# Chunk-selected attention and a hard-swish layer: K and Q of the quads in longer rows, bounds in three column groups, batch 0's high bounds in four, a new order

## The chip, the cores and the metric

The kernel runs on one core of one Trainium2 chip. The metric is the device time of one execution in microseconds; for each kernel the median of several runs is given. A profiled execution gives the trace from which the views of the profile are taken.

## What is computed

Attention over 4 batches, 8 heads, 768 tokens of 64 elements, in which each query attends to at most 6 chunks of 32 keys, followed by a layer without biases. Per head:

```python
k_min, k_max = k_chunks.min(axis=3), k_chunks.max(axis=3)      # 24 chunks of 32 keys
ub = sum(maximum(q * k_min, q * k_max), axis=-1)               # an upper bound for each query and chunk
ub = where(chunk of the query >= chunk, ub, -1e9)
sel = the 6 chunks with the highest ub
scores = where(sel & causal, scale * q @ k.T, -1e9)
out = softmax(scores) @ v
```

The heads are put side by side (3,072 rows of 512), and then

```python
h = x @ w_in                                                   # 512 -> 2048
y = (h * clip(h + 3, 0, 6) / 6) @ w_out                        # 2048 -> 512
```

The first 192 queries see at most 6 chunks, so no selection is needed for them; bounds and masks are made for queries 192 to 767.

## The kernel before

**Order.** One list of tokens, `ORDER`, is walked once (line 660). Each token calls one function, which issues the instructions of one step. A token names the step, its numbers, and the PSUM buffer that it writes: a, b, c are two banks each (`PSB`), x and y one bank each (`PSS`; a, b and c can serve so too). Each engine runs its instructions in the order in which they were issued and waits on semaphores for what they read and for buffers to be free. The list therefore fixes the order on each engine and on each DMA queue, SP's above all.

**Batch 0, pairs of heads** (tokens in capitals). A pair i has 128 partitions, 64 for each head. K and Q are loaded by halves of 384 tokens (`LK`, `LQ`, `AQ`, 96 KB each), turned on TensorE (`KT`, `QT`), reduced to chunk maxima and minima on VectorE (`MX`, `MN`), cast on ScalarE (`KB`, `QB`). The bounds are two products, of the positive part of q (`RP`) with the maxima and of the negative part (`RN`) with the minima: `UH.i.h`, with h 0 for the first 192 queries that need a selection and 1 for the other 384. Then a bias add (`UB`), a turn on TensorE (`TH`), the eight largest (`T8`), the comparison with the sixth (`SE`), the turn back (`LH`), and a copy (`MT`). `S` computes scores in six units, to which a matmul with a constant adds -8192 where a chunk was not chosen.

**Batches 1 to 3, quads of heads** (small letters; n is 2 to 7, four heads on 32 partitions each). `lk.n` and `lq.n` load K and Q, four DMAs of 192 KB each: partition t of a head gets tokens t, t+32, t+64 and so on, in rows of 256 bytes. `kd` and `qd` turn 32x32 blocks on VectorE in place, so that 32 elements of the head dimension lie along partitions. Each step has two halves. `mx` and `mn` reduce K to chunk maxima and minima, and `kx` subtracts them; `kb` and `qb` cast to bf16 on ScalarE; `rp` makes the positive part of q. With max(q a, q b) = q b + relu(q)(a - b), the bounds (`ud.n.c.cc`) are 64 small matmuls in 4 row and 4 column groups of the TensorE array, 144 queries in each column group. After them come, for two heads at a time, bias add (`us`), turn (`tr`), top-8 (`tm`, nine `max`), comparison (`se`) and turn back (`tb`), all on VectorE, and then `mv.n.g`, GpSimd copies that bring the rows of head g to its 32 partitions. `SQ.n.u` computes scores and mask of the four heads for unit u.

**All batches.** `ex` exponentiates scores on ScalarE, `af` applies the causal mask on GpSimd, `A` and `B` multiply by the values (low and high half), `na` and `nb` normalise on VectorE. x is turned into `XT` by TensorE (`X`, with the copy `xe` on VectorE) or by DMA transposes on SP's queue (`xt`). Per group g of 384 rows, `H.g.f` are eight blocks of 8 matmuls with `w_in`, `hu` and `gt` the gate on ScalarE and VectorE, `O.g.t.n` four blocks of 4 matmuls with `w_out` for each of three tiles, `ot` the eviction and `st` the store. Weights are loaded by `wl` and cast on GpSimd by `wc`; values by `LV`/`VC` and `lv`/`vc`.

**Staging.** K and Q of the quads share three slabs of `STAGE`; a load waits until everything that read the slab's last content is done.

Of the kernel before, what the change touches and what calls it, by code (L numbers as in the profile page):

```python
# [15 lines left out]
P = 128  # L16
# [30 lines left out]
KB.3.1 S.3.1.b ex.3.1 S.3.0.c LQ.3.1.0 LV.1.0.0 LQ.3.1.1 QT.3.1.x MX.3.1 RN.3.1 ex.3.0 VC.1.0 af.2.0 A.1.y na.1
RP.3.1 LH.2.1.b MT.2.1 S.1.3.a ex.1.3 S.1.4.c LV.2.0.0 kd.2.1 X.0.0.y xe.0.0 ex.1.4 UH.3.1.b UB.3.1 af.3.1 mx.2.1
S.1.5.a S.1.2.c QB.3.1 VC.3.0 af.3.0 A.3.y na.3 LV.2.0.1 ex.1.5 af.1.3 ex.1.2 VC.2.0 A.2.x S.0.2.b ex.0.2 TH.3.1.y
na.2 S.2.3.c ex.2.3 T8.3.1 LV.0.1.1 SE.3.1 wl.0 S.2.5.a X.0.1.x xe.0.1 S.2.2.b ex.2.2 LH.3.1.y MT.3.1 wc.0 af.0.2  # L50
wl.1 kd.2.0 mx.2.0 H.0.1.c hu.0.1 ex.2.5 gt.0.1 mn.2.0 af.1.2 af.0.3 LV.0.1.0 VC.0.1 B.0.0.x H.0.0.b hu.0.0 gt.0.0
wc.1 B.0.1.x nb.0 H.0.2.c hu.0.2 mn.2.1 gt.0.2 S.3.3.b ex.3.3 S.3.2.a ex.3.2 LV.1.1.1 LV.1.1.0 VC.1.1 kb.2.1 af.1.5
kb.2.0 wl.2 wc.2 B.1.0.y B.1.1.y nb.1 lk.3 S.3.5.b af.3.2 kd.3.1 mn.3.1 bd ex.3.5 af.3.5 H.0.4.c hu.0.4 gt.0.4
mx.3.1 H.0.3.a S.2.4.b af.2.2 ex.2.4 kd.3.0 kx.2 mx.3.0 wl.3 H.0.5.c hu.0.5 gt.0.5 hu.0.3 af.2.5 lq.2 gt.0.3 wc.3
H.0.6.b hu.0.6 S.3.4.c qd.2.1 af.3.3 ex.3.4 LV.3.1.0 H.0.7.a gt.0.6 af.2.3 rp.2.1 qd.2.0 LV.3.1.1 VC.3.1 LV.2.1.1
X.1.0.c xe.1.0 B.3.0.x LV.2.1.0 B.3.1.x kb.3.0 VC.2.1 B.2.0.y B.2.1.y nb.3 rp.2.0 ud.2.c.b nb.2 hu.0.7 wl.4 gt.0.7
X.1.1.x xe.1.1 H.1.3.a hu.1.3 us.2.1 qb.2.0 us.2.0 tr.2.1 H.1.1.b hu.1.1 tm.2.1 wc.4 mn.3.0 O.0.0.0.y se.2.1 gt.1.3
gt.1.1 tb.2.1 mv.2.3 lq.3 qd.3.0 qd.3.1 wl.5 H.1.6.c kb.3.1 hu.1.6 gt.1.6 O.0.2.0.x tr.2.0 kx.3 H.1.5.a hu.1.5
qb.2.1 wc.5 mv.2.2 H.1.2.b hu.1.2 rp.3.1 gt.1.5 H.1.0.c rp.3.0 O.0.0.1.y gt.1.2 tm.2.0 hu.1.0 gt.1.0 O.0.2.1.x
qb.3.0 wl.6 wc.6 se.2.0 ud.3.b.a tb.2.0 mv.2.1 mv.2.0 us.3.1 tr.3.1 H.1.7.c hu.1.7 lv.5 wl.7 us.3.0 lk.4 H.1.4.a  # L60
wc.7 hu.1.4 vc.5 gt.1.7 tm.3.1 O.0.2.2.x SQ.2.5.c.b lq.4 ex.5.5 gt.1.4 qb.3.1 O.0.0.2.y SQ.2.4.b.a ex.4.5 af.4.5
ex.5.4 se.3.1 tb.3.1 mv.3.3 O.0.2.3.x ot.0.2 tr.3.0 tm.3.0 O.0.0.3.y se.3.0 tb.3.0 ex.4.4 mv.3.1 kd.4.1 mx.4.1
ot.0.0 SQ.2.0.a.c ex.4.0 kd.4.0 mn.4.0 ex.5.0 mv.3.2 mv.3.0 O.0.1.0.x O.0.1.1.x qd.4.1 SQ.2.3.b.a O.0.1.2.x ex.5.3
qd.4.0 lv.4 ex.4.3 O.0.1.3.x ot.0.1 SQ.2.1.c.a ex.4.1 af.4.1 st.0.0 O.1.0.0.y O.1.0.1.y lv.7 rp.4.1 ex.5.1
SQ.2.2.c.b O.1.0.2.y vc.4 af.5.5 rp.4.0 ex.5.2 mn.4.1 mx.4.0 kx.4 af.4.3 af.4.0 A.4.x na.4 af.5.0 qb.4.0 st.0.1
ex.4.2 ud.4.b.a af.5.1 kb.4.0 st.0.2 af.5.2 us.4.0 O.1.0.3.y us.4.1 vc.7 tr.4.1 ot.1.0 tm.4.1 SQ.3.1.c.b O.1.2.0.x
ex.7.1 ex.6.1 kb.4.1 SQ.3.0.a.b se.4.1 ex.6.0 lv.6 ex.7.0 lk.5 tr.4.0 tm.4.0 A.5.y O.1.2.1.x SQ.3.4.c.a af.6.1
ex.7.4 vc.6 af.6.0 na.5 A.6.y O.1.2.2.x na.6 af.4.2 tb.4.1 kd.5.1 af.7.1 SQ.3.3.a.b ex.6.4 lv.8 af.7.0 ex.6.3 A.7.y
X.2.0.c O.1.2.3.x xe.2.0 ex.7.3 SQ.3.5.a.c ot.1.2 na.7 ex.6.5 X.2.1.b xe.2.1 B.4.0.x B.4.1.x af.5.3 B.5.0.y kd.5.0
se.4.0 mx.5.0 ex.7.5 mn.5.0 B.5.1.y qb.4.1 mv.4.3 H.2.2.b nb.5 nb.4 H.2.0.a hu.2.2 hu.2.0 gt.2.2 st.1.0 H.2.3.c  # L70
# [41 lines left out]
def kernel(  # L112
# [104 lines left out]
    def load_rows(m, x):  # L217
        def issue(n, *only):
            b, first = divmod(4 * n, H)
            dst = staged(m, n).rearrange("p h n x t -> p (h n) (x t)")  # L220
            for g in only or range(4):
                nc.sync.dma_start(dst[CH * g:CH * (g + 1)], x[b, first + g].rearrange("(n t) d -> t n d", t=CH))
# [470 lines left out]
```

## Time and profile before

| what | us |
|---|---|
| median of 3 runs | 278.69 (277.73 to 280.13) |
| the profiled execution | 275.69 |
| its span, first to last instruction | 274.0 |
| TensorE busy in it | 261.3 |
| VectorE busy | 184.0 |
| ScalarE busy | 181.0 |
| GpSimd busy | 102.6 |

The granted clock of TensorE was 1.000 over the whole span. A busy time counts an instruction from its start to its end, and matmuls overlap, so the busy time of TensorE is not a measure of its peak. Line numbers (L333) are those of the kernel before; PE, DVE, ACT, POOL and SP are TensorE, VectorE, ScalarE, GpSimd and the sync engine; PEld is the loading of weights, and a q behind an engine means its sequencer or queue. The moved bytes were 36.08 MB in 91,479 DMA packets, 84,144 of them under 512 bytes.

### The profile page before, as it was taken

The numbers are of one execution on the slowest core, as the hardware profiler recorded it, in microseconds if no ns is written. First come the engines' busy times: TensorE is split into PE (matmuls) and PEld (weight loads), VectorE is DVE, ScalarE is ACT, GpSimd is POOL, SyncE is SP. The second block draws the span as 40 slices with busy tenths as digits, with TensorE's granted clock in tenths as the row PEclk, the third lists the DMA queues.
The fourth block names the chain that finished last, engine by engine and source line by source line (L and its number), as shares of the span: only waits on it lengthen the run. The fifth ranks groups of instructions, "written<-read, shape, count | busy, mean of one in ns | idle before, by whom it ended". The sixth has DMA issues, their size and how long they took to land.

```text
span 274.0 us, 8574 instructions
## 1 busy us (share of the span) xinstructions
PE 261.3 (95%) x3550; PEld 153.7 (56%) x3550; DVE 184.0 (67%) x452; ACT 181.0 (66%) x249; POOL 102.6 (37%) x241
## 2 busy tenths in 40 slices
PE   6998997899999999999999999998999999999994
PEld 3666765565545565664545655464655565555561
DVE  4898998999899779867874788575662423342620
ACT  2798978647499894878578746992887634325610
POOL 7215686325777552532825232421544310000000
PEclk9999999999999999999999999999999999999999
DMA  8999999998996999139900449114212044003002
GB/s 164 205 180 163 335 250 252 219 286 246 261 184 190 160 212 186 36 76 171 231 4 28 107 103 173 40 21 99 79 52 47 2 133 100 0 2 115 38 22 97
DMA packets 91479, 36.08 MB, mean 132 GB/s; under 512 B 84144, under 2 KB 84400, under 8 KB 91440
## 3 DMA queue, kind: packets, MB, share of 16 engines
q1 hardware_dynamic: 89040, 34.94, 56.6%
q10 hardware_dynamic: 2400, 0.59, 1.2%
q8 instruction: 28, 0.46, 0.8%
q14 instruction: 11, 0.09, 0.1%
HBM read 27.26 MB, written 6.29 MB: 122 GB/s over the span
## 4 chain that ended last, share of the span: by engine, by line
PE 76%; DMA 13%; SPq 3%; DVE 3%; POOL 1%; ACT 1%; issue 1%; DVEq 0%
PE PSy L625 15%; PE PSx L625 10%; PE PBa L587 10%; PE PBc L587 9%; PE PBb L587 8%; DMA WS<-in_moe_w_in_dram 4%; DMA STAGE<-in_q_dram 4%; DMA STAGE<-in_k_dram 3%; PE PBa L510 3%; PE PSx L543 2%; PE PSy L543 2%; PE PBc L625 2%; PE PBc L510 2%; PE PBb L510 2%; PE PBb L333 2%; DMA XT<-XB 1%
## 5 line engine op out<-in xcount | busy, mean ns | idle before, releaser
L587 PEld LDWEIGHTS <-WIN 128*128 128x128 bf16 x512 | 48.9, 98 | 37.7 <-issue 4.2
L527 POOL TENSOR_SCALAR_AFFINE_SELECT PT<-PT 128x256 bf16<-128x256 bf16 x78 | 30.2, 409 | 70.2 <-ACT PT L520 69.9
L625 PEld LDWEIGHTS <-GT 128*128 128x128 bf16 x368 | 33.1, 98 | 37.8 <-issue 2.4
L625 PE MATMUL PSy<-WOUT,GT 128*128 128x512 bf16 x192 | 46.8, 380 | 0.0
L363 POOL COPY MQ<-MTM 32x144 bf16<-32x144 bf16 x96 | 29.1, 304 | 31.3 <-DVE MTM L357 27.5
L587 PE MATMUL PBc<-XT,WIN 128*128 128x384 bf16 x184 | 33.7, 326 | 1.4 <-DVE GT L598 1.4
L598 DVE SCALAR_TENSOR_TENSOR GT<-U,PBa 128x768 bf16<-128x768 bf16 x22 | 20.9, 948 | 19.8 <-ACT U L595 19.8
L587 PE MATMUL PBa<-XT,WIN 128*128 128x384 bf16 x176 | 32.4, 326 | 1.3 <-DMA XT<-XB 0.7
L625 PE MATMUL PSx<-WOUT,GT 128*128 128x512 bf16 x128 | 31.8, 380 | 0.0
L598 DVE SCALAR_TENSOR_TENSOR GT<-U,PBc 128x768 bf16<-128x768 bf16 x23 | 21.8, 947 | 10.4 <-ACT U L595 10.3
L520 ACT ACTIVATE PT<-PBb 128x1024 bf16<-128x1024 f32 (+2 forms) x26 | 23.6, 908 | 7.6 <-PE PBb L514 5.3
L587 PE MATMUL PBb<-XT,WIN 128*128 128x384 bf16 x152 | 27.8, 326 | 0.2 <-POOL WIN L242 0.2
L595 ACT ACTIVATE U<-PBc 128x768 bf16<-128x768 f32 x23 | 18.7, 812 | 13.9 <-PE PBc L587 10.2
L598 DVE SCALAR_TENSOR_TENSOR GT<-U,PBb 128x768 bf16<-128x768 bf16 x19 | 18.1, 951 | 13.6 <-ACT U L595 13.6
L595 ACT ACTIVATE U<-PBa 128x768 bf16<-128x768 f32 x22 | 17.9, 812 | 13.5 <-PE PBa L587 13.5
L520 ACT ACTIVATE PT<-PBc 128x1024 bf16<-128x1024 f32 (+2 forms) x26 | 24.2, 930 | 3.5 <-PE PBc L497 1.3
L520 ACT ACTIVATE PT<-PBa 128x1024 bf16<-128x1024 f32 (+2 forms) x26 | 23.9, 921 | 3.8 <-PE PBc L514 2.0
L228 DVE STREAM_TRANSPOSE STAGE<-STAGE 128x768 f32<-128x768 f32 x24 | 22.7, 960 | 1.7 <-DMA STAGE<-in_k_dram 1.3
L595 ACT ACTIVATE U<-PBb 128x768 bf16<-128x768 f32 x19 | 15.4, 812 | 12.1 <-PE PBb L587 12.1
L311 DVE TENSOR_REDUCE KMA<-STAGE 128x24 f32<-128x768 f32 x24 | 22.3, 941 | 0.1
L543 PEld LDWEIGHTS <-PT 128*128 128x128 bf16 x546 | 19.0, 97 | 3.6 <-issue 0.7
L510 PEld LDWEIGHTS <-KBA 32*128 32x128 bf16 x480 | 9.4, 92 | 14.7 <-issue 11.7
(192 smaller groups left out, 460.3 us busy)
## 6 DMA issues: line engine op xcount, KB each, us to landing
out_dram<-OT SPq DMA_DIRECT2D x23, 256.0 KB, 2.5
STAGE<-in_k_dram SPq DMA_DIRECT2D x24, 192.0 KB, 5.0
STAGE<-in_q_dram SPq DMA_DIRECT2D x24, 192.0 KB, 5.5
VS<-in_v_dram SPq DMA_DIRECT2D x12, 384.0 KB, 4.2
WS<-in_moe_w_in_dram SPq DMA_DIRECT2D x4, 1024.0 KB, 7.0
WS<-in_moe_w_out_dram SPq DMA_DIRECT2D x4, 1024.0 KB, 6.7
STAGE<-in_k_dram SPq DMA_DIRECT2D x16, 96.0 KB, 3.2
VS<-in_v_dram SPq DMA_DIRECT2D x16, 96.0 KB, 4.2
```

The source lines that it names most:

```text
L228: nc.vector.transpose(out=T, in_=T)
L311: nc.vector.tensor_reduce(out=dst, in_=staged("k", n)[:, h], axis=AX.X, op=(A.max, A.min)[w])
L333: nc.tensor.matmul(PSB[(c, cc)[g // 2]][CH * part:CH * (part + 1), g % 2, 0:NQ // 4], lhsT=KM4[n % 2][rows, w, x, :], rhs=R[rows, :, x, 8 ...
L363: nc.gpsimd.tensor_copy(MQ[n % 2][CH * g:CH * (g + 1), w * part:w * (part + 1)], MT4[n % 2][CH * part:CH * (part + 1), w * g:w * (g + 1)])
L510: nc.tensor.matmul(PSB[both[g // 2]][:, g % 2, at:at + w], lhsT=K[rows, x, j * P:(j + 1) * P], rhs=Q[rows, x, q0:q0 + w], start=(x == 0), ...
L520: nc.scalar.activation(pt(i, u)[:, :, 0:n], PSB[slot["S", i, u]][:, :, 0:n], ACT.Exp, scale=float(scale))
L527: nc.gpsimd.affine_select(out=T[:, :, lo:lo + P], in_=T[:, :, lo:lo + P], pattern=[[0, 2], [1, P]], compare_op=A.is_ge, fill=0.0, base=0, ...
L543: nc.tensor.matmul(O[:, e, t, :], lhsT=pt(i, u)[:, e, lo:lo + P], rhs=VB[i % 4][:, j, e, :], start=(j == 0), stop=(j == qb))
L587: nc.tensor.matmul(PSB[c][:, ff, 0:GRP], lhsT=WIN[:, kt, (2 * f + ff) * P:(2 * f + ff + 1) * P], rhs=XT[g % 3][:, kt, :], start=(kt == 0), ...
L595: nc.scalar.activation(slot["R", g, f][:], PSB[slot["H", g, f]][:, :, 0:GRP], ACT.Relu, bias=3.0)
L598: nc.vector.scalar_tensor_tensor(out=GT[g % 2][:, 2 * f:2 * f + 2, :], in0=slot["R", g, f][:], scalar=6.0, in1=PSB[slot["H", g, f]][:, :, ...
L625: nc.tensor.matmul(PSS[c], lhsT=GT[g % 2][:, f, t * P:(t + 1) * P], rhs=WOUT[:, f, :], start=(f == 0), stop=(f == FT - 1))
```

## The change

- Quads: K is loaded with 4 consecutive tokens a partition (rows of 1,024 bytes), Q with 6 (1,536 bytes). After the turn the tokens lie in another order, which each reader takes into account: `kb` and `qb` are two casts of half the size instead of one, and write tokens 4 or 6 elements apart; `mx` and `mn` are two reduces, over two axes.
- Bounds of the quads: three column groups of 192 queries instead of four of 144, so 48 matmuls instead of 64, whose right-hand sides are contiguous. Bias add, turn, comparison and turn back work on 96 partitions and 384 columns (before 128 and 288), top-8 has 12 `max` a step instead of 9, and the turn is made in place. `mv.n.g` is 3 copies of 192 that put the queries back in order, instead of 4 of 144; the mask matmul then reads contiguous columns.
- Batch 0, h = 1: bounds in four column groups of 96 (16 matmuls instead of 8), a bias add on 128 partitions and 192 columns (before 64 and 384), two turns instead of four.
- The order is new throughout. The low half of batch 1's x (group 2) is turned by `xt.2`, DMA transposes, where before it was `X.2.0`, `X.2.1` on TensorE with two copies on VectorE. `bd`, the bias of the quads, is now among the first steps. Otherwise the list has the same steps.

```diff
+    RUN = {"k": 4, "q": 6}
+    NP3 = NQ // 3
+    def slab(m, n):
+        at = (1 + 2 * (n - FIRST_QUAD) + "kq".index(m)) % 3
+        return FLAT[:, 2 * S * at:2 * S * (at + 1)]
     def staged(m, n):
-        at = (1 + 2 * (n - FIRST_QUAD) + "kq".index(m)) % 3
-        return STAGE[:, 2 * at:2 * at + 2].rearrange("p h (n x t) -> p h n x t", x=2, t=CH)
+        return slab(m, n).rearrange("p (u r x t) -> p x u r t", r=RUN[m], x=2, t=CH)
...
-                nc.sync.dma_start(dst[CH * g:CH * (g + 1)], x[b, first + g].rearrange("(n t) d -> t n d", t=CH))
+                nc.sync.dma_start(dst[CH * g:CH * (g + 1)], x[b, first + g].rearrange("(u t r) d -> t u (r d)", t=CH, r=RUN[m]))
...
+    def first_query(h, g):
+        return Q0 * (h + 1) + (96, Q0)[h] * (g % 2) + 96 * (g // 2)
...
-            dst = (KB4 if m == "k" else QB4)[n % 2][:, :, SH * h:SH * (h + 1)].rearrange("p x (n t) -> p n x t", t=CH)
...
+            dst = (KB4 if m == "k" else QB4)[n % 2].rearrange("p x (u t r) -> p x u r t", t=CH, r=RUN[m])
+            n_u = S // (2 * CH * RUN[m])
+            for x in range(2):
+                out, src = dst[:, x, n_u * h:n_u * (h + 1)], staged(m, n)[:, x, n_u * h:n_u * (h + 1)]
...
     def chunk_bounds(w):
         def issue(n, h):
-            dst = KM4[n % 2][:, w, :, NCH // 2 * h:NCH // 2 * (h + 1)].rearrange("p x n -> p n x")
-            nc.vector.tensor_reduce(out=dst, in_=staged("k", n)[:, h], axis=AX.X, op=(A.max, A.min)[w])
+            for x in range(2):
+                src = staged("k", n)[:, x, 3 * h:3 * h + 3].rearrange("p u r (c t) -> p u c r t", t=CH // RUN["k"])
+                dst = KM4[n % 2][:, w, x, NCH // 2 * h:NCH // 2 * (h + 1)].rearrange("p (u c) -> p u c", c=4)
+                nc.vector.tensor_reduce(out=dst, in_=src, axis=AX.XY, op=(A.max, A.min)[w])
...
-                for part in range(4):
+                for part in range(3):
                     for g in range(4):
                         rows = slice(CH * g, CH * (g + 1))
-                        nc.tensor.matmul(PSB[(c, cc)[g // 2]][CH * part:CH * (part + 1), g % 2, 0:NQ // 4],
-                                         lhsT=KM4[n % 2][rows, w, x, :], rhs=R[rows, :, x, 8 * part:8 * part + 8],
+                        R = raw[rows, x, part + 1] if w else RPA[rows, x, NP3 * part:NP3 * (part + 1)]
+                        nc.tensor.matmul(PSB[(c, cc)[g // 2]][CH * part:CH * (part + 1), g % 2, 0:NP3],
+                                         lhsT=KM4[n % 2][rows, w, x, :], rhs=R,
...
-        for s in range(9):
-            nc.vector.max(out=T8D[:, 9 * p + s, :], in_=bounds_rows(p)[:, s, :])
+        for s in range(12):
+            nc.vector.max(out=T8D[0:96, 12 * p + s, :], in_=bounds_rows(p)[:, s, :])
...
-        for part in range(4):
-            w = NQ // 4
-            nc.gpsimd.tensor_copy(MQ[n % 2][CH * g:CH * (g + 1), w * part:w * (part + 1)],
-                                  MT4[n % 2][CH * part:CH * (part + 1), w * g:w * (g + 1)])
+        for part in range(3):
+            lo = NP3 * part
+            nc.gpsimd.tensor_copy(MQ[n % 2][CH * g:CH * (g + 1), lo:lo + NP3].rearrange("p (t r) -> p r t", t=CH),
+                                  MT3[(2 * n + g // 2) % 3][CH * part:CH * (part + 1), NP3 * (g % 2):NP3 * (g % 2 + 1)]
+                                  .rearrange("p (r t) -> p r t", t=CH))
...
     def bounds_half(i, h, c):
-        n = 96 * (h + 1)
         for m, R in enumerate((RP, RN)):
-            for g in range(2):
-                lo = Q0 * h + n * g
+            for g in range(2 * (h + 1)):
+                lo = first_query(h, g) - Q0
...
-                                 rhs=chosen[rows, (lo - Q0) // CH:(q0 + w - Q0) // CH], start=False, stop=True,
+                                 rhs=MQ[n % 2][rows, lo - Q0:q0 + w - Q0], start=False, stop=True,
```

The part of the new order around the bounds of quad 4, as the prediction speaks of it:

```diff
-SQ.2.2.c.b O.1.0.2.y vc.4 af.5.5 rp.4.0 ex.5.2 mn.4.1 mx.4.0 kx.4 af.4.3 af.4.0 A.4.x na.4 af.5.0 qb.4.0 st.0.1
-ex.4.2 ud.4.b.a af.5.1 kb.4.0 st.0.2 af.5.2 us.4.0 O.1.0.3.y us.4.1 vc.7 tr.4.1 ot.1.0 tm.4.1 SQ.3.1.c.b O.1.2.0.x
+af.4.1 mv.3.3 kb.4.0 kb.4.1 af.5.3 tb.3.0 mv.3.0 mv.3.1 vc.6 mn.4.1 mn.4.0 O.1.0.0.y O.1.0.1.y lv.7 mx.4.1 vc.7
+mx.4.0 kx.4 ud.4.b.a kd.5.1 mx.5.1 qb.4.0 af.4.5 us.4.1 O.1.0.2.y SQ.3.1.a.c A.4.x ex.6.1 af.6.1 tr.4.1 ex.7.1
+us.4.0 SQ.3.0.a.b na.4 ex.6.0 af.5.1 A.5.x O.1.0.3.y na.5 mn.5.1 ex.7.0 ot.1.0 st.0.0 af.4.3 SQ.3.4.a.c af.6.0
```

More of the change, by code (lines that the diff above doesn't have):

```diff
@@ L208 @@
     IDENTB = const.tile([P, P], BF16, name="IDENTB")
[L209 to L211 removed]
+    BIASM = const.tile([P, 2, 96], FP32, name="BIASM")
+    BIASH = [BIASM[0:64, 0], BIASM[:, 1]]
+    BIAS3 = const.tile([96, NP3], FP32, name="BIAS3")
     EM = const.tile([P, NBLK, 2, P], BF16, name="EM")
```

243 lines of the change are left out of this document (118 added, 125 removed).

## Prediction

> **What bounds the kernel now.** I read the page first, then the windows, the chain of waits, and last single groups and stretches of the timeline. On the page the share of TensorE says how little there can be to win, and the slices say where.
>
> ```profile
> span 274.0 us, 8574 instructions
> PE 261.3 (95%) x3550; PEld 153.7 (56%) x3550; DVE 184.0 (67%) x452; ACT 181.0 (66%) x249; POOL 102.6 (37%) x241
> DVE  4898998999899779867874788575662423342620
> DMA  8999999998996999139900449114212044003002
> GB/s 164 205 180 163 335 250 252 219 286 246 261 184 190 160 212 186 36 76 171 231 4 28 107 103 173 40 21 99 79 52 47 2 133 100 0 2 115 38 22 97
> ```
>
> TensorE is busy 95% of the span. A slice is 6.85 us: in the first 13 (to 89 us) VectorE and the DMA engines are also near full, and after that both fall off. I cut the windows at the events that matter below.
>
> ```profile
> 0.00:9.84 9.84, 6.78 (x50) 4.25 (x53) 5.10 (x21) 3.60 (x8) 7.14 (x17) 1.00 1.00 180
> 9.84:40.00 30.16, 28.57 (x470) 20.05 (x460) 29.05 (x105) 25.70 (x42) 13.71 (x27) 1.00 0.95 229
> 40.00:52.42 12.42, 9.76 (x114) 6.20 (x114) 10.58 (x17) 9.57 (x12) 7.33 (x12) 1.00 1.09 220
> 52.42:60.00 7.58, 7.15 (x217) 5.52 (x216) 7.07 (x14) 3.18 (x6) 2.90 (x3) 1.00 1.12 271
> 60.00:89.22 29.22, 29.22 (x386) 15.25 (x390) 27.22 (x70) 22.91 (x32) 19.67 (x45) 1.00 0.90 229
> 89.22:259.85 170.63, 169.94 (x2282) 96.90 (x2282) 103.11 (x227) 114.05 (x149) 51.83 (x139) 1.00 0.42 89
> ```
>
> Columns: length, then PE, PEld, DVE, ACT and POOL busy, granted clock, DMA share, GB/s. From 89 us on TensorE lacks 0.7 us of 170.6 while VectorE is 60% busy: there only TensorE's own work counts. Up to 89 us three things are full at once. Which one decides is in the chain of waits, and in what VectorE waited for:
>
> ```profile
> 44.62 7.67 DMA STAGE<-in_q_dram
> 52.42 0.98 DVE STAGE L228
> 55.73 0.31 PE PBc L333 x2
> ```
> ```profile
> DVE STAGE L228 <- DMA STAGE<-in_k_dram: 1.3, 1, 1.3
> DVE STAGE L228 <- DMA STAGE<-in_q_dram: 0.5, 1, 0.5
> ```
>
> The first quad's Q lands at 52.29 us, is turned on VectorE, and its bounds start on TensorE at 55.73. So the chain runs through the loads, but VectorE, which the data goes to, waited for them only 1.8 us in all. It had other work. That is the point of this case: the loads are late, but VectorE is nearly as full as they are.
>
> **The loads (gain, mostly covered).** Before 52.29 us three quad loads of 4 x 192 KB run (K of quads 2 and 3, Q of 2): 2.36 MB in 256-byte rows. At the 180 GB/s of the first window, where all is 256-byte rows, that is 13.1 us; at the 335 GB/s of the fifth slice, which has 2,048-byte weight rows in it, 7.0. Longer rows lie between, so 3 to 6 us of DMA time go. The new order issues four 96 KB V loads ahead of quad 2's Q that stood behind it (0.39 MB, 2.1 us at 180), so this Q lands 1 to 4 us earlier. SP gains too:
>
> ```profile
> 42.00 4.87 SPq L222 DMA_DIRECT2D STAGE<-in_q_dram  x4
> ```
>
> These four issues held SP's queue for 4.87 us, with V loads and w_out behind them. None of it ends the kernel by itself: what it can give is VectorE's wait for data, 1.8 us. More than that, up to all of VectorE's idle time, needs the order to refill it.
>
> **VectorE ahead of quad 4 (loss).** Take the subtract of quad 4's chunk bounds (`kx.4`), after which its bounds go to TensorE (`ud.4`). In both orders the same list of VectorE steps stands ahead of it, only permuted, so its time changes by the new costs and by idle time alone.
>
> ```profile
> 87.98 0.46 DVE L316 TENSOR_TENSOR KMA<-KMA 128x48 f32<-128x48 f32 x1
> 89.16 0.31 PE L333 MATMUL PBb<-RPA,KMA 32*32 32x144 f32 x2
> ```
> ```profile
> L311 DVE TENSOR_REDUCE KMA<-STAGE 128x24 f32<-128x768 f32 x24 | 22.3, 941 | 0.1
> 13.59 1.01 DVE L412 TENSOR_REDUCE KMA<-PBb 128x12 f32<-128x384 f32 x2
> L350 DVE MAX8 T8D<-UBT 128x8 f32<-128x32 f32 x108 | 11.0, 176 | 0.3
> L446 DVE TENSOR_TENSOR UBM<-PBa,BIASM 64x384 f32<-64x384 f32 x2 | 1.1, 547 | 0.3 <-PE PBa L440 0.3
> L446 DVE TENSOR_TENSOR UBM<-PBa,BIASM 64x192 f32<-64x192 f32 x2 | 0.7, 342 | 0.0
> ```
>
> - Chunk max and min: 12 steps ahead of `kx.4` become two reduces of 384 each. Two such take 1.01 us (batch 0's row), one of 768 takes 22.3/24 = 0.93: +0.08 x 12 = +1.0 us. By full durations it would be +1.9.
> - Top-8: two quads of 18 become 24: 12 more at 11.0/108 = 0.10, +1.2 us.
> - Bias add, both turns and select: 16 steps go from 288 to 384 columns. 192 columns more cost 547 - 342 = 205 ns, so 96 cost 0.10: +1.6 us.
> - Batch 0's high bounds: four bias adds go from 64x384 to 128x192: -0.2 x 4 = -0.8 us.
>
> Sum +3.0 us (to +3.9). Against it the 1.8 us of data waits: `kx.4` ends at 88.44 + 3.0 - 1.8 = 89.6 us. VectorE's idle time from 9.84 us to there is 1.11 + 1.84 + 0.51 + 2.00, less the 0.8 us between 88.44 and 89.22: 4.7 us. So the ends are 88.44 + 3.0 - 4.7 = 86.7 and 88.44 + 3.9 = 92.3.
>
> **TensorE's own work.**
>
> ```profile
> 69.92 0.31 PE L333 MATMUL PBb<-RPA,KMA 32*32 32x144 f32 x2
> 70.17 0.29 PE L333 MATMUL PBa<-RPA,KMA 32*32 32x144 f32 x2
> 71.87 1.47 PE L587 MATMUL PBc<-XT,WIN 128*128 128x384 bf16 x8
> 98.89 0.34 PE PBc L576 x6
> 100.69 0.44 PE PBb L576 x6
> 61.26 0.86 PE PSy L625 x4
> 88.86 0.36 PE PSx L543 x12
> ```
>
> A quad's bounds take 71.87 - 69.92 = 1.95 us. The new form has 48 matmuls of 192 columns for 64 of 144: the columns are the same, the instructions a quarter fewer. By columns it stays 1.95, by instructions 1.46. I take 1.8: the first 32 of 128 recorded starts lie within 69.92 to 70.17, 8 ns each, and all 128 take 15 each, so the engine can issue twice as fast as it then does, and the columns set most of the pace. Those of quads 2 and 3, and the shorter batch-0 bounds and turns, lie ahead of `ud.4` and are covered by VectorE's lateness; uncovered they would give about 1 us. Quads 4 to 7 give 4 x 0.15 = 0.6. The transposes of group 2 (0.34 + 0.44 = 0.78) leave TensorE for DMA transposes. A projection block (0.86) and a values block (0.36) that stood ahead of `ud.4` now follow it: +1.2.
>
> ```profile
> 183.02 1.20 SPq L569
> 185.58 4.07 DMA XT<-XB
> PE PBa L587 <- DMA XT<-XB: 0.7, 1, 0.7
> PE PBc L625 <- DVE GT L598: 0.4, 2, 0.3
> ```
>
> DMA transposes take 6.6 us from first issue (183.02) to landing (189.65). Group 2's have about 10 us of matmuls before their first use. Group 5's, which cost 0.7 us before, now have some 9 us: -0.7. Group 7's follow the last normalise with about 6: +0.5. At the end two waits for the gate, 0.7 us with what follows, go, as three projection blocks now cover them: -0.7. New waits stand behind `ud.4`: on VectorE a turn (0.98) and two reduces (1.01) of quad 5 come ahead of quad 4's bias adds, so its second score buffer is free 2.0 + 0.55 + 0.57 + 0.55 = 3.7 us after `ud.4` starts (add, turn, add), and TensorE wants it after 1.8 + 0.86 + two short blocks of some 0.4, at 3.4; the second values block then waits for the normalise of the first: +0.4.
>
> **ScalarE and GpSimd.**
>
> ```profile
> L303 ACT CAST KBA<-STAGE 128x768 bf16<-128x768 f32 x12 | 9.9, 832 | 0.0
> L363 POOL COPY MQ<-MTM 32x144 bf16<-32x144 bf16 x96 | 29.1, 304 | 31.3 <-DVE MTM L357 27.5
> ```
>
> Each cast becomes two of 384, at half of 832 ns plus a start; I take +0.15 us a cast, 3.6 us over all 24, in ScalarE's 6.3 idle us of 60 to 89 and more later. Row gathers go from 16 of 144 to 12 of 192, near equal; GpSimd is 37% busy. Quad biases now lead GpSimd's queue, ahead of the identity that the first transposes read:
>
> ```profile
> L369 POOL TENSOR_SCALAR_AFFINE_SELECT BIAS<-BIAS 32x144 f32<-32x144 f32 x4 | 1.7, 421 | 0.1
> 1.32 3.06 DMA STAGE<-in_k_dram
> 4.41 3.41 DMA STAGE<-in_q_dram
> ```
>
> Three selects of 192, about 0.45 each, 1.4 us, stand beside loads that land at 4.4 to 7.8; without that cover they would cost the 1.4. The rest (order of stores, table sizes) I cost at nothing: it lies after 89 us beside a full TensorE.
>
> The casts now write bf16 4 (K) and 6 (Q) elements apart, which no row here shows. [...] From rows alone: between no change and twice the 832 ns.
>
> **Sum.** `ud.4` at 89.7 us. What followed it took 274.0 - 89.16 = 184.8; now 184.8 + 1.2 - 0.8 - 0.6 - 0.7 + 0.4 - 0.7 + 0.5 = 184.1. Span 273.8, -0.2 us. The profiled execution took 275.69, 1.7 more than its span; the median of the runs is 278.69. The difference on the median gives 278.5; I set 279.2, 0.7 more, for small waits of the new order that sums by engine don't find. Its own range, with `kx.4` up to 1.5 us to either side and the bounds at 1.46 or 1.95, is 276.5 to 282.
>
> **Rivals.**
> - *The loads decide (faster).* For it: DMA share about 1.0 to 60 us, and the chain. Against: VectorE waited 1.8 us for them. If the order refills all 4.7 us, `ud.4` comes at 86.7 instead of 89.7; with bounds at 1.46 another 4 x 0.34 = 1.4 goes: 276.2 to 274.8 us.
> - *Strided casts (slower).* ScalarE evicts the scores, and a cast stands ahead of those in its queue. Ahead of `ud.4` are 8 Q and K casts from 60 us on or just before; at twice the duration they add 8 x 0.8 = 6.6 us against 6.3 idle us, most of which TensorE ends. It decides once a pair of casts is above about 1.6 us, where the idle time is used up; what TensorE feels of it I put at half to three quarters, 3 to 5 us: 282 to 284.
> - *The order pays for VectorE (slower).* No idle time is saved, reduces cost their full duration (`kx.4` at 92.3, +2.6), and the quads after it, each 1.8 us dearer on VectorE, delay masks by another 1 to 2 us: 283 to 284. For it: VectorE 27.2 of 29.2 us before 89.22. Against: 60% after.
> - *The rows bring no speed.* Then the 1.8 us of waits stay: 281.
>
> **Chances.** Own forecast 0.45, loads decide 0.25, casts 0.08, order pays 0.14, rows no faster 0.08. About 1% (2.8 us) is what a measurement tells from no change. Faster by that (under 275.9): most of the first rival and the edge of my own, 0.25. Slower (over 281.5): the casts, the order, half of the rows, a tenth of my own, 0.33. Within: 0.42. The range reaches from the loads' case to the two slow ones: 274.5 to 284.5.
>
> **What would show it.** Right: quad loads at over 1.5 times the old rate; Q of quad 2 landed by 51 us; VectorE over 95% busy to 89 us; `ud.4` between 88.5 and 91 us, directly behind the subtract of quad 4's bounds; bounds between 1.46 and 1.95 us; casts near 0.5 us. Wrong: `ud.4` at 87 with VectorE idle (TensorE's path), casts over 0.8 us for 384, or new idle time of TensorE after 92 us of more than 2 us.

## The result and the profile after

| what | before | after |
|---|---|---|
| median of 4 runs each, us | 278.21 (277.33 to 280.13) | 307.81 (307.0 to 312.98) |
| ratio, 95% interval | | 1.104 (1.097 to 1.112) |
| the profiled execution, us | 275.69 | 307.0 |
| from the first matmul of quad 4's bounds (`ud.4`) to the end of the span, us | 184.8 | 206.9 |
| TensorE's mean granted clock | 1.000 | 0.964 |

The change made the kernel 29.6 us slower; the forecast was 279.2 us, with 284.5 us as the upper end of the range. The slowest run of the changed kernel, 312.98 us, is of a slow state and stands outside the ratio. The page of the changed kernel:

```profile
span 305.0 us, 8328 instructions
...
PE 268.7 (88%) x3402; PEld 154.8 (51%) x3402; DVE 191.1 (63%) x510; ACT 213.7 (70%) x273; POOL 132.7 (44%) x218
...
PE   5398997989799599798959999759998999999994
...
q1 hardware_dynamic: 61488, 35.33, 47.8%
...
PE 47%; ACT 13%; DVE 12%; POOL 10%; issue 6%; DMA 5%; SPq 5%; ACTq 1%; DVEq 0%; POOLq 0%
```

The rows of the page are busy time, TensorE's 40 slices, the main DMA queue and the chain that ended last, by engine. VectorE grew by 7 us, ScalarE by 33 and GpSimd by 30, and TensorE, which before was full in all slices from 9 to 39 but one, now falls short in nine of them, the last being slice 31. The chain was 76% TensorE's; now 23% of it are ScalarE's and GpSimd's. The main queue's packets took 47.8% of 305.0, 146 us of 16 engines, where they took 56.6% of 274.0, 155 us: the longer rows did save time there. The groups that carry the growth:

```profile
L376 POOL COPY MQ<-MTM 32x192 bf16<-32x192 bf16 x72 | 59.1, 821 | 30.5 <-DVE MTM L370 27.5
...
L311 ACT CAST QBA<-STAGE 128x384 bf16<-128x384 f32 x24 | 33.2, 1603 | 0.0
...
L231 DVE STREAM_TRANSPOSE STAGE<-STAGE 128x768 f32<-128x768 f32 x24 | 22.7, 959 | 3.2 <-DMA STAGE<-in_q_dram 3.2
L321 DVE TENSOR_REDUCE KMA<-STAGE 128x12 f32<-128x384 f32 x48 | 23.4, 540 | 0.2
L311 ACT CAST KBA<-STAGE 128x384 bf16<-128x384 f32 x24 | 23.0, 1125 | 0.0
...
STAGE<-in_k_dram SPq DMA_DIRECT2D x24, 192.0 KB, 3.5
STAGE<-in_q_dram SPq DMA_DIRECT2D x24, 192.0 KB, 5.0
```

A cast of half the size takes 1,603 ns (Q) or 1,125 ns (K), where one of the full size took 832 ns. A gather takes 821 ns where it took 304. The last two rows are the quads' loads, with their size and the us from issue to landing. TensorE now waits for both, and for one thing at the start:

```profile
PE PBc L599 <- DVE GT L610: 5.3, 4, 1.7
PE PBc L453 <- ACT RPA L436: 5.2, 1, 5.2
PE PBb L526 <- POOL MQ L376: 4.0, 2, 3.1
...
PE PBa L522 <- ACT PT L532: 2.7, 1, 2.7
PE PBa L526 <- POOL MQ L376: 2.7, 2, 2.2
PE PBc L526 <- POOL MQ L376: 1.9, 1, 1.9
```

These are TensorE's waits: the line that waits, the releaser, us in total, times, the longest. L599 is a block of `w_in`, which waits for a gate to free its buffer (1.4 us before); L453 are batch 0's bounds; L526 is the mask matmul, which reads the gathered rows; L522 is a score block, which waits for its PSUM buffer to be evicted by ScalarE. How a cast gets between a gate and TensorE is seen in the chain (start, us, what):

```profile
120.05 1.05 ACT KBA L311 x2
121.10 0.42 ACT OT L644
121.52 4.65 ACT QBA L311 x4
126.17 0.17 issue
126.34 1.07 ACT RPA L332
127.41 0.70 ACT U L607
128.13 0.96 DVE GT L610
129.14 0.97 PE PBc L599 x5
```

The four casts of one quad's Q follow each other for 4.65 us on ScalarE; the gate (`U`, then `GT` on VectorE) stands behind them in its queue, and TensorE's next block of `w_in` waits for the buffer that the gate reads.

The 5.2 us at the start come from ScalarE's queue:

```profile
8.76 0.21 ACT L248 ACTIVATE TINY<-TINY 1x8 f32<-1x8 f32 x1 [3.54 <-DVE TINY L254]
11.83 0.44 ACTq L393 DMA_DIRECT2D STAGE<-in_q_dram  x1
12.32 0.48 ACT L419 CAST KBA<-PBa 128x384 bf16<-128x384 f32 x1 [3.35 <-DMA STAGE<-in_q_dram]
```

The new order puts `AQ.2.0.0`, a load of Q that ScalarE issues, behind loads on SP's queue and directly ahead of batch 0's first evictions. The chain has this issue behind a load of Q that SP issued at 9.14 us and that landed at 11.81: it goes out at 11.83 us, and the evictions behind it wait with it: the first ends at 12.8 us. What ties the one load to the other no view shows. TensorE stood idle from 8.3 to 13.5 us, and its granted clock was 0.50 between 10 and 20 us.

The clock has a part in the loss. Of the 31.0 us by which the span grew, 23.6 are time without a matmul (12.7 us before, 36.3 after) and 7.4 are busy time of TensorE (261.3 and 268.7). The granted clock was 0.50 from 9.8 to 20.0 us, and for 3.4 us each from 84.9, 105.4 and 160.0 us on; TensorE was busy in 16.8 of these 20.4 us. The last three begin within 1 us of the end of a wait of 1.9 to 2.7 us. Not every wait has this behind it: the one of 3.1 us that ended at 205.8 us has not.

### The profile page after: what moved, and what is told of

Same layout as the page of the kernel before. It is cut to its first block, busy times and chain, and to the rows that moved or that the text cites. A ratio compares the mean times of both kernels' runs of the same rounds, so it can differ in the third digit from the quotient of the medians.

```text
span 305.0 us, 8328 instructions
## 1 busy us (share of the span) xinstructions
PE 268.7 (88%) x3402; PEld 154.8 (51%) x3402; DVE 191.1 (63%) x510; ACT 213.7 (70%) x273; POOL 132.7 (44%) x218
## 3 DMA queue, kind: packets, MB, share of 16 engines
q1 hardware_dynamic: 61488, 35.33, 47.8%
## 4 chain that ended last, share of the span: by engine, by line
PE 47%; ACT 13%; DVE 12%; POOL 10%; issue 6%; DMA 5%; SPq 5%; ACTq 1%; DVEq 0%; POOLq 0%
POOL MQ L376 9%; PE PSx L637 7%; PE PSy L637 7%; PE PBc L599 7%; DMA STAGE<-in_q_dram 4%; PE PBa L599 4%; ACT QBA L311 3%; ACT KBA L311 3%; DVE GT L610 3%; PE PSy L555 3%; ACT PT L532 3%; ACT U L607 3%; SPq L581 2%; PE PBb L637 2%; PE PBb L522 2%
## 5 line engine op out<-in xcount | busy, mean ns | idle before, releaser
L376 POOL COPY MQ<-MTM 32x192 bf16<-32x192 bf16 x72 | 59.1, 821 | 30.5 <-DVE MTM L370 27.5
L599 PEld LDWEIGHTS <-WIN 128*128 128x128 bf16 x512 | 49.6, 99 | 44.8 <-issue 12.8
L599 PE MATMUL PBc<-XT,WIN 128*128 128x384 bf16 x224 | 42.3, 333 | 7.0 <-DVE GT L610 5.3
L637 PE MATMUL PSx<-WOUT,GT 128*128 128x512 bf16 x176 | 43.9, 383 | 0.0
L532 ACT ACTIVATE PT<-PBb 128x1024 bf16<-128x1024 f32 (+2 forms) x32 | 29.6, 926 | 9.9 <-PE PBa L526 6.6
L637 PE MATMUL PSy<-WOUT,GT 128*128 128x512 bf16 x128 | 33.3, 396 | 0.5 <-ACT OT L627 0.5
L311 ACT CAST QBA<-STAGE 128x384 bf16<-128x384 f32 x24 | 33.2, 1603 | 0.0
L599 PE MATMUL PBa<-XT,WIN 128*128 128x384 bf16 x176 | 32.2, 326 | 1.0 <-DVE GT L610 1.0
L321 DVE TENSOR_REDUCE KMA<-STAGE 128x12 f32<-128x384 f32 x48 | 23.4, 540 | 0.2
L311 ACT CAST KBA<-STAGE 128x384 bf16<-128x384 f32 x24 | 23.0, 1125 | 0.0
L599 PE MATMUL PBb<-XT,WIN 128*128 128x384 bf16 x112 | 20.5, 326 | 0.4 <-DVE GT L610 0.4
L522 PE MATMUL PBa<-QBA,KBA 32*128 32x384 bf16 (+2 forms) x172 | 17.5, 286 | 3.7 <-ACT PT L532 2.7
```

What stands on the lines that cost most here:

```text
L311: nc.scalar.copy(out, src)
L321: nc.vector.tensor_reduce(out=dst, in_=src, axis=AX.XY, op=(A.max, A.min)[w])
L376: nc.gpsimd.tensor_copy(MQ[n % 2][CH * g:CH * (g + 1), lo:lo + NP3].rearrange("p (t r) -> p r t", t=CH), MT3[(2 * n + g // 2) % 3][CH * pa ...
L522: nc.tensor.matmul(PSB[both[g // 2]][:, g % 2, at:at + w], lhsT=K[rows, x, j * P:(j + 1) * P], rhs=Q[rows, x, q0:q0 + w], start=(x == 0), ...
L532: nc.scalar.activation(pt(i, u)[:, :, 0:n], PSB[slot["S", i, u]][:, :, 0:n], ACT.Exp, scale=float(scale))
L599: nc.tensor.matmul(PSB[c][:, ff, 0:GRP], lhsT=WIN[:, kt, (2 * f + ff) * P:(2 * f + ff + 1) * P], rhs=XT[g % 3][:, kt, :], start=(kt == 0), ...
```

## Experiments

Each kernel was run once with a profile, beside the kernel before on the same chip (275.6 to 277.2 us there), unless more runs are told. Single times are compared with the profiled execution of the changed kernel, 307.0 us. "Packed" means that elements are written next to each other; where the text does not say that the step went to the reading side, such a kernel leaves out the reordering, so that scores or mask columns of the quads belong to other tokens, and it serves for its time alone. Differences of 1 to 2 us between single runs carry little: 13 runs of the kernel before on one chip lie between 275.5 and 277.0 us.

**The price of a step in the address (p1).** Copies by themselves, appended to the kernel before, three of each, on ScalarE with write steps of 1, 2, 3, 4, 6, 8 and 16 elements, on GpSimd of 1, 2, 4 and 6, and some with the step on the reading side. Of each engine one is shown:

```diff
+    def every(T, step, n):
+        return T[:, 0:step * n].rearrange("p (n s) -> p s n", s=step)[:, 0]
+    nc.scalar.copy(every(PROBE, 6, 384), FLAT[:, 0:384])
+    nc.gpsimd.tensor_copy(every(SMALL, 6, 192)[0:32], MQ[0][0:32, 0:192])
```

> The kernel before, and behind its last store a row of copies with nothing beside them: 384 elements from fp32 to bf16 on ScalarE, written 1, 2, 3, 4, 6, 8 and 16 elements apart, then read 2, 4 and 8 fp32 elements apart, then in K's and Q's own pattern with the step on the reading side and packed writes; 192 bf16 elements on GpSimd the same way, and three on VectorE. Theory 'the step of the write sets the price': 0.5 us packed, 1.1 us at 4 elements (8 bytes) and 1.6 at 6 (12 bytes), also with nothing beside them; GpSimd 0.35 packed, 0.8 at 6. Rival 'contention': alone all of them take about 0.5 us, and the 1.1 and 1.6 came from what ran beside them. What a step costs on the reading side is open: near packed (0.5) if only writes pay, 1 us or more if both do.

The groups of that run, L671 to L676 with write steps of 1, 4, 6 and 8 elements of 2 bytes on ScalarE, L683 with K's pattern on the reading side, and on GpSimd L685 with step 1, L688 with 6, L689 with the gather's order on the reading side:

```profile
L676 ACT CAST GT<-STAGE 128x384 bf16<-128x384 f32 x3 | 5.7, 1888 | 0.1
L675 ACT CAST GT<-STAGE 128x384 bf16<-128x384 f32 x3 | 4.4, 1466 | 0.1
L674 ACT CAST GT<-STAGE 128x384 bf16<-128x384 f32 x3 | 3.1, 1045 | 0.1
L683 ACT CAST GT<-STAGE 128x384 bf16<-128x384 f32 x3 | 2.5, 839 | 0.1
L688 POOL COPY GT<-MQ 32x192 bf16<-32x192 bf16 x3 | 2.4, 813 | 0.2
L671 ACT CAST GT<-STAGE 128x384 bf16<-128x384 f32 x3 | 1.5, 509 | 0.1
L689 POOL COPY GT<-MQ 32x192 bf16<-32x192 bf16 x3 | 1.5, 497 | 0.2
L685 POOL COPY GT<-MQ 32x192 bf16<-32x192 bf16 x3 | 1.3, 426 | 43.5 <-PE PSy L613 43.3
```

The prices of the changed kernel are nearly there in copies that have no neighbour: 1,045 and 1,466 ns for 4 and 6 elements, where the casts of the changed kernel took 1,125 and 1,603, and 813 ns for the gather, which took 821. (The copy of the gather's step in GpSimd's first round and ScalarE's last two rounds have nothing beside them; the rounds agree within 2%.) So it is the step that sets the price; what ran beside the casts has added 8 to 9% at most. Up to 8 elements, 16 bytes, each element adds to it: 8 take 1,888 ns, 3.7 times the packed 509, and 16 take no more (1,795). (L685's mean holds its first copy; e2 below has 340 ns for the packed gather.) The same reordering on the reading side costs less: 839 ns for K's cast, 497 ns for the gather.

Against the packed copies, ScalarE's write 8 bytes apart took twice the time (1,045 and 509 ns). On GpSimd L689, which reads 64 bytes apart, is 46% above the 340 ns (497), and L688, which writes 12 bytes apart, is 139% above them (813).

**Casts packed, gathers packed, both (e1, e2, e4).**

```diff
-            dst = (KB4 if m == "k" else QB4)[n % 2].rearrange("p x (u t r) -> p x u r t", t=CH, r=RUN[m])
+            dst = (KB4 if m == "k" else QB4)[n % 2].rearrange("p x (u r t) -> p x u r t", t=CH, r=RUN[m])
```
```diff
-            nc.gpsimd.tensor_copy(MQ[...][..., lo:lo + NP3].rearrange("p (t r) -> p r t", t=CH),
-                                  MT3[...][...].rearrange("p (r t) -> p r t", t=CH))
+            nc.gpsimd.tensor_copy(MQ[...][..., lo:lo + NP3], MT3[...][...])
```

> The changed kernel, but both casts of the quads write packed, in the order in which the slab holds the tokens, so the scores of the quads belong to other tokens. Theory 'strided casts': ScalarE's casts fall from 56 us in all to about 24, and the time from 308 to 285 to 293. Rival 'the order': the casts get cheap and the time stays above 300. Rival 'gathers and start': 300 to 305.

> The changed kernel, but the row gathers on GpSimd write packed, so the mask columns of the quads stay in the slab's order. Theory 'strided casts first, gathers second': 72 gathers fall from 0.82 to about 0.35 us each (59 to 25 us), TensorE's waits for them (8.6 us) go, the time falls to 297 to 303. Rival 'gathers are off the path': within 2 us of 308. Rival 'gathers are the main cause': below 292.

> Casts and gathers both write packed rows, in a wrong order of tokens; everything else is as in the changed kernel. Theory (the steps in the writes are one joint cost: whichever of the two is mended, TensorE then waits for the other): together they give more than the 3.4 us and 7.8 us of the two single edits, that is 290 us or less against 307 us. Rival (the two costs add, and most of the loss is the order or VectorE's longer steps): about 307 - 11 = 296 us.

Casts alone packed: 304.4 us, casts at 518 and 527 ns. Gathers alone: 300.1 us, 340 ns. Both: 285.2 us. The single edits give 2.6 and 7.0 us (3.4 and 7.8 beside the median of the changed kernel), both together 21.8. The waits of e1 show why the first gave so little:

```profile
PE PBb L526 <- POOL MQ L376: 4.8, 3, 3.1
PE PBc L453 <- ACT RPA L436: 4.6, 1, 4.6
PE PBa L526 <- POOL MQ L376: 4.2, 2, 2.2
...
PE PBc L526 <- POOL MQ L376: 1.9, 1, 1.9
```

TensorE's waits for gathers grew from 8.6 to 10.9 us: what ScalarE no longer held, GpSimd did. The two slow engines stood side by side ahead of the same scores, and each covered most of the other. The additive rival (296 us) is out. All of this is from one run of each, but 21.8 us lie far outside the spread of the runs.

**The step on the reading side (e7, e11).** The elements end where the changed kernel puts them, so the result is that of the reference; e11 is in the order of the kernel before.

```diff
-            dst = (...)[n % 2].rearrange("p x (u t r) -> p x u r t", t=CH, r=RUN[m])
+            dst = (...)[n % 2].rearrange("p x (u t r) -> p x u t r", t=CH, r=RUN[m])
...
-                out, src = dst[...], staged(m, n)[:, x, ...]
+                out, src = dst[...], staged(m, n)[:, x, ...].rearrange("p u r t -> p u t r")
```

> The changed kernel, with the step on the reading side: casts and gathers read in steps of 128 or 64 bytes and write packed rows, with the same result. By the prices measured apart, 0.84 us for either cast and 0.49 us a gather, ScalarE saves 24 x (1.60 - 0.84) + 24 x (1.13 - 0.84) = 25 us of busy time and GpSimd 72 x (0.82 - 0.49) = 24 us. Theory (the joint cost of the steps): about three quarters of what packed rows throughout give, 292 to 296 us. Rival (costs add): 298 to 300 us.

> The changed functions in the order of the kernel before, with the step on the reading side as in e7, the same result as the reference. By e7, which won back 15 of the 22 us that packed rows win: two thirds of what e10 wins, 312.3 - 18 = 294 us. Rival (the order, as for e10): 300 us or more.

e7: 292.4 us, two thirds of what packed rows give; casts and gathers as p1 priced them, within 7%:

```profile
L376 POOL COPY MQ<-MTM 32x192 bf16<-32x192 bf16 x72 | 36.4, 505 | 33.6 <-DVE MTM L370 30.6
...
L311 ACT CAST KBA<-STAGE 128x384 bf16<-128x384 f32 x24 | 19.6, 895 | 0.0
```

e11: 286.2 us, 8 us better than expected and the fastest of the kernels that do all that the changed one does, still 10 us behind the kernel before.

**The order (e3, e5, e10).** e3 is the changed functions in the order of the kernel before, e5 the functions before in the new order, e10 as e3 with packed writes.

> All new steps (longer rows, strided casts and gathers, three column groups, four in batch 0) in the order of the kernel before. Theory 'the steps' own prices': 295 to 305, the 5 us lost at the start come back and the rest stays. Rival 'the new order': 278 to 284. If it is slower than the changed kernel (over 309), the new order was of help to these steps.

> The functions of the kernel before, with the new order. Theory (the new order costs little but the start, where ScalarE's queue stands behind a late transfer of Q and TensorE idles 5.2 us): 280 to 285 us. Rival (the new order itself is the loss): 295 us or more.

> The changed functions in the order of the kernel before, casts and gathers written in packed rows (tokens in a wrong order). Theory (the steps of the writes make most of the 312.3 us that the changed functions take in this order): 285 us or less, 27 us off, as in the new order, where they made 22 us. Rival (the old order does not fit the new steps, whatever the writes cost): 295 us or more.

312.3, 288.5 and 282.3 us. The new order is not the loss: with strided writes the old one is 5 us worse, and without them both come to 282 us once the start is mended (e8). Packing gives 30 us in the old order, 22 in the new. e5 lies between its two expectations, 12.8 us above the kernel before on its chip.

**The start (e6, e8, e9, e14).** `LQ` for `AQ` lets SP issue the load: in the changed kernel (e6), with packed writes (e8), with the functions before (e9). e14 is e8 with `PW`, the clearing of the tile `WARM`, ahead of the other clearings.

```diff
-LQ.0.1.1 RN.1.0 EG.0 AQ.2.0.0 KB.1.0 EG.2 QB.0.0 ...
+LQ.0.1.1 RN.1.0 EG.0 LQ.2.0.0 KB.1.0 EG.2 QB.0.0 ...
```

> The changed kernel, where one transfer of Q, half 0 of pair 2, is issued by SP instead of ScalarE. Theory (TensorE's idle stretch of 5.2 us from 8.3 us on stands on the path and is nothing but ScalarE's queue held by that transfer's issue): TensorE starts its bounds by 9 us instead of 13.5 us and the time falls by 4 to 6 us to 301 to 303 us. Rival (TensorE catches up later, since it has idle time in every stretch): 305 to 308 us.

> Packed casts and gathers as in e4, and the transfer of Q issued by SP as in e6. Theory (once the steps are gone, TensorE is nearly full behind the start, so that what the start loses is no longer made up): the 2.9 us that TensorE's first 20 us gained in e6 come through, 285.2 - 3 = 282 us, or up to 4.5 us less. Rival (a later wait, the loads of Q behind SP's queue, takes it back as in e6): 284.5 us or more.

> The functions of the kernel before in the new order, with the transfer of Q issued by SP. Theory (288.5 us is the start's loss, and an order that was laid out for other steps): 284 to 286 us, the rest, some 9 us, being the order. Rival (the start is all of it): 276 to 278 us.

> As e8, with the clearing of the warm-up tile put first on VectorE, as the kernel before has it. Theory (TensorE's first matmul at 3.1 us instead of 1.3 us costs nothing, since its first transposes wait for K and Q and the identity until 5.5 us in both): 282 us, no change. Rival (the later warm-up is part of what is left): 280.5 us.

e6: TensorE's wait of 5.2 us fell to 1.3, and the time stayed at 307.5 us. The gain was there, for `ud.4` starts at 94.4 us instead of 98.1, and was lost behind it, where what follows took 211.0 us instead of 206.8. TensorE's idle time there grew from 16.8 to 19.0 us, and the granted clock was 0.50 for 20.5 us instead of 6.8. e8: 282.4 us, 2.9 less than e4. e9: 282.2 us, 6.3 less than e5. So the loss at the start is worth 3 to 6 us where no strided write follows; where they follow, e6 shows nothing of it in the time. e14: 282.8 us, no gain.

**VectorE's added work (e12, e13).** The minimum over K's second 32 columns left out, 12 reduces, in e8 and in e10.

```diff
-            for x in range(2):
+            for x in range(2 - w):
```

> As e8, and of the quads' 48 reduces the 12 that take the minimum over K's second 32 columns are left out, so that those bounds stay as they were: 12 x 0.54 = 6.5 us less on VectorE, whose busy time is then that of the kernel before (184 us). Theory (VectorE's added work ahead of each quad's bounds holds the rest): half of the 6.6 us or more goes, 276 to 279 us. Rival (the rest is the order and the start, VectorE has room): 281 us or more.

> As e10, the changed functions with packed writes in the order of the kernel before, with the same 12 reduces left out. Theory (VectorE's added work): 276 to 279 us against 282.3 us. Rival (the order does not fit): 281 us or more.

280.9 and 280.7 us: 1.5 and 1.6 us off, near the rival, and about the spread of single runs, so that the size is uncertain. The end of quad 4's subtract (`kx.4`) moved more; the rows are of e10 and e13:

```profile
93.80 0.25 DVE L326 TENSOR_TENSOR KMA<-KMA 128x48 f32<-128x48 f32 x1
```
```profile
91.56 0.45 DVE L326 TENSOR_TENSOR KMA<-KMA 128x48 f32<-128x48 f32 x1
```

Six of the twelve reduces, 3.2 us, lie ahead of it, and it ends 2.0 us earlier: VectorE's work there has a part in setting it, about 0.6 us a microsecond in this pair of runs.

**Batch 0's four groups alone (e15), a longer stream alone (e16, e17).** e15 is the kernel before with `bounds_half`, `bias_half`, `turn_half` and the tables of the changed one. e16 and e17 add to the kernel before 24 or 48 matmuls at the start:

```diff
             nc.tensor.matmul(PSB[c][:, 0, :] if c in PSB else PSS[c], lhsT=WARM[:, 0:P], rhs=WARM, start=True, stop=True)
+        for _ in range(24):
+            nc.tensor.matmul(PSS[c][0:CH, 0:8], lhsT=WARM[:, 0:CH], rhs=WARM[:, 0:8], start=True, stop=True)
```

> The kernel before, in its own order, with batch 0's high bounds in four column groups and nothing else of the change. By the prediction's terms the high halves' transposes lose 0.8 us of TensorE and VectorE's biasing some tenths, in a stretch where DMA and VectorE are nearly full: 275 to 277 us beside the before of the same chip, no change that can be measured. Rival (TensorE's 64 more small matmuls a pair cost more than the transposes give): 278 us or more.

> The kernel before, with 24 matmuls of 8 columns behind the 6 that warm TensorE at the start, where it stands idle for 1.5 us; nothing else is changed, and nothing reads them. Theory (what e15 lost comes from a longer stream of TensorE instructions, whose places against the loading of its code move): 278 to 281 us, with an idle stretch of a microsecond or more for no shown reason. Rival (it comes from the changed lengths of the high bounds' steps against an order laid out for others): 276 us, as before.

> As e16 with 48 matmuls of 8 columns. Theory: 278 to 281 us, the idle stretch at another place than in e16. Rival: 276 us, or up to 1 us more where they end after TensorE's idle stretch.

| kernel | median, us (runs) | ratio to before, 95% interval |
|---|---|---|
| e15 | 280.69 (10) | 1.013 (1.009 to 1.016) |
| e16 | 282.41 (4) | 1.017 (1.011 to 1.024) |
| e17 | 279.69 (6) | 1.009 (1.006 to 1.013) |

All three are slower, with intervals that lie above 1, though none clearly by 2%; VectorE's busy time in e15 is no longer than before (183.6 us, 184.0 before). The 64 more matmuls of e15's expectation are 32 in all, 8 for each pair (64 rows of the trace). The 24 and 48 matmuls took 0.76 and 1.44 us, in an idle stretch of 1.5. Each trace has an idle stretch of TensorE of about 2.4 us for which it shows no reason; the rows are of e15, e16 and e17, from the timeline:

```profile
60.26 0.31 PE L335 MATMUL PBc<-STAGE,KMA 32*32 32x144 f32 x2 [2.37 <-issue]
```
```profile
95.14 0.81 PE L627 MATMUL PSy<-WOUT,GT 128*128 128x512 bf16 x3 [2.52 <-issue]
```
```profile
59.92 0.31 PE L335 MATMUL PBc<-STAGE,KMA 32*32 32x144 f32 x2 [2.35 <-issue]
```

In e15 and e17 it lies in the middle of one quad's bounds, in e16 in a block of `w_out`; the kernel before has none of that kind. A load of code stands where each begins; this is e15's, in the DMA view of 57 to 58 us:

```profile
q8 instruction: 1, 0.02, 8.4%
```

The kernel before has such a load at 58 to 59 us too, without the idle time. So the length of the stream moves the time, by 2.5 to 5 us here.

The same kind of stretch also stands behind a name. The first row is of the kernel before, the others are of e10:

```profile
PE PBa L587 <- DVE XT L580: 0.3, 1, 0.3
```
```profile
PE PBa L598 <- DVE T8D L363: 3.0, 1, 3.0
...
59.18 0.56 DVE L591 COPY XT<-PSx 128x768 bf16<-128x768 bf16 x1 [0.65 <-PE PSx L587]
```

The third matmul of this block of `w_in` needs the copy of x (`XT`). In the kernel before it starts at 58.83 us, 0.05 us after that copy. In e10 the copy ends at 59.74 us and the matmul starts at 62.44; the top-8 (`T8D`), which the profile names because it ended last, is nothing that it reads. So 2.7 us of this wait have no reason either. e13 and e16 have such a wait at the same block (3.07 and 2.31 us, ending at 61.11 and 60.36 us), and e8, e12 and e14 one ahead of a block of `w_in` (1.58, 2.58 and 2.53 us), where the copies of x and the bias add that frees its buffer were done 1.8 us or more before it ends. In all of these and in the three rows above TensorE goes on 2.5 to 3.0 us after a load of code began. In e10, e15, e16 and e17 the granted clock was 0.50 for the next 3.4 us (from 62.7, 61.2, 96.1 and 61.6 us on), where the kernel before has 1.00, so that such a stretch costs more than its own length: in e15 the 8 matmuls of a block of `w_in` took 2.89 us from 61.04 us on, and 1.46 us at 66.32. Why TensorE stood idle in these stretches no run shows.

## Why the prediction was wrong

The mechanism that decided was in the prediction as a rival, "Strided casts (slower)", with a chance of 0.08 and 282 to 284 us. The step that failed is the term "+0.15 us a cast, 3.6 us over all 24" and, for the rival, its bound "between no change and twice the 832 ns". Two casts took 2.25 us (K) or 3.2 us (Q) in place of one of 832 ns: 46 us more by durations (24 x 1.125 + 24 x 1.603 - 24 x 0.832), where the term had 3.6 and the bound allowed 20. Both were the author's estimates; the prediction itself says that no row shows such a write. ScalarE's busy time, which counts overlapped instructions once (56.2 us for the 48 casts, 65.5 by durations), grew by 33.

By its other steps:

- *"Row gathers go from 16 of 144 to 12 of 192, near equal"*: missed altogether. The same step of 12 bytes stands in the gather's write. 12 x 0.821 = 9.9 us a quad instead of 16 x 0.304 = 4.9. The prediction saw the strided write in the casts and did not look for it in the copies that put queries back in order, and so it had one slow engine where there were two, each covering the other (e1, e2, e4).
- *"what TensorE feels of it I put at half to three quarters"*: packing took 31 us off ScalarE (213.7 to 182.6) and 35 off GpSimd (132.7 to 98.0), and TensorE felt 22 us of these 66 (e4), a third.
- *"The rest (order of stores, table sizes) I cost at nothing"*: of the start it priced GpSimd's queue and not ScalarE's, past which `AQ.2.0.0` was moved. That cost 3 to 6 us where nothing later covered it.
- *The loads*: the transfers did get shorter, K's quads from 5.0 to 3.5 us from issue to landing, Q's from 5.5 to 5.0. But VectorE's 1.8 us of data waits did not go; the row of the turns has 3.2 us of them after the change.
- *"`kx.4` ends at 88.44 + 3.0 - 1.8 = 89.6 us"*: it ended at 95.88 in the changed kernel. With packed writes, order and start as before (e10) it ended at 94.05, still 4.5 us late. e12 and e13 give VectorE's sum its share. Another part is in no sum by engine: e10 has its wait of 2.97 us and the 3.4 us at a clock of 0.50 ahead of `kx.4`, and e15 and e17, whose like stretches lie there too, have it at 92.12 and 92.35 us without added work on VectorE.
- *"`ud.4` at 89.7 us, then 184.1"*: with packed writes and the start mended (e8) 92.9 and 187.4; in the changed kernel 98.1 and 206.9. So 8.4 us of the miss of 31.2 lie ahead of `ud.4` and 22.8 behind, where the text had "only TensorE's own work counts". That was read from VectorE's share before the change and carried over to ScalarE and GpSimd. There two casts became 2.7 to 3.9 times as long as the one before, and a gather 2.7 times.
- *Bounds "I take 1.8"*: measured as there, from the first start to the start of the next block, quad 4's took 99.97 - 98.11 = 1.86 us instead of 1.95. The columns set nearly all of it; a quarter fewer instructions gave 0.09 of the 0.49 us that they could have given.
- Of the marks that it named as showing it wrong, two came: casts over 0.8 us for 384, and new idle time of TensorE after 92 us of more than 2 us.

The account of the 31.3 us between the profiled executions, 275.7 and 307.0 us: strided writes of casts and gathers 21.8 (e4), the start 2.9 more (e8). Of the 6.6 us that are left, about 1.5 go with 12 of VectorE's reduces (e12, e13), within the spread of single runs. Batch 0's four groups alone cost 3.5 us (e15), and as much as that comes from a longer TensorE stream by itself (e16, e17). How much of the 6.6 us is that effect stays open. It has a part: e8 has a wait of 1.58 us and e10 one of 2.97 us of that kind, with a clock of 0.50 behind e10's. e8's longest wait, 2.82 us at 44.6 us, is of the order: the gate stands on VectorE behind a turn of K that waited 2.4 us for its load. The quads' dearer top-8 and turns, the three column groups and the longer rows were not tried alone.

## What to carry to other kernels

Where a layout change makes a transfer cheaper by reordering elements, look up every instruction that puts the order back, and price its step on the side where the step falls: here the write side cost twice to four times the packed copy (1,045 to 1,888 ns against 509 on ScalarE, 813 against 340 on GpSimd), the reading side about one and a half times (839 against 509, 497 against 340). If two engines become slow ahead of the same consumer, mending one shows less than its part (2.6 and 7.0 us alone, 21.8 together here); undo both before ruling either out. And where the list of instructions has been fitted closely, expect that an edit which changes the length of TensorE's stream can cost something by that alone: three such edits of this kernel cost 0.9 to 1.7%. When the profile names a releaser, look whether the waiting instruction reads or overwrites anything of it.

## What the runs showed of the hardware

- ScalarE, 384 fp32 to bf16: 0.51 us packed, 0.62 with a write step of 4 bytes, 0.83 with 6, 1.05 with 8, 1.47 with 12, 1.89 with 16, and 1.80 with 32. A read step of 16 bytes costs less: 0.86 us.
- GpSimd, 192 bf16 on 32 partitions: 0.34 us packed, 0.60 with a write step of 8 bytes, 0.81 with 12.
- A load that ScalarE issued went out at 11.83 us, 0.02 us after one that SP had issued landed, and ScalarE's first cast behind it was held with it: ScalarE was idle for 3.35 us ahead of that cast.
- 24 matmuls of 8 columns in an idle stretch at the start made the kernel 1.7% slower, with idle stretches of TensorE of 2.3 us at 58 us, 2.0 of it without a reason in the trace, and of 2.5 us at 93 us, all without one.
- The granted clock of TensorE was 0.50 for 3.4 us behind idle stretches of 2.35 to 2.97 us (e10, e15, e16, e17), but not behind one of 3.1 us in the changed kernel at 205.8 us, nor behind the one of 2.3 us in e16 at 60.4 us.
